# Reordering the work around one late load, and reading 64 bytes of every 64 KB of two weight matrices early

## The chip, the cores and the metric

The kernel runs on one core of one Trainium2 chip. The metric is the device time of one execution in microseconds (us), lower is better. Kernels are compared only within the same rounds.

## The reference

Eight batches of linear attention with a cosine weighting of positions, then one feed-forward layer with a gated activation. Only the shapes and the formulas matter here.

```python
q, k, v: (8, 8, 576, 64)      # batch, heads, sequence, head dim
r_c, r_s = relu(x) * cos(theta), relu(x) * sin(theta)      # phi(x) = [r_c, r_s]
kv  = einsum('bhsf,bhsd->bhfd', phi(k), v);  z = phi(k).sum(axis=2)
num = einsum('bhsf,bhfd->bhsd', phi(q), kv)
x   = num / (einsum('bhsf,bhf->bhs', phi(q), z) + 1e-6)    # -> (4608, 512)
h   = x @ w_in                        # w_in 512 x 2048
g   = h * sigmoid(beta * h)
out = g @ w_out                       # w_out 2048 x 512
```

## The kernel before

The tokens go through the feed-forward layer in nine chunks of 512. A chunk has 32 slots: 16 with the four matmuls of one h tile each, 16 with four output ("o") matmuls each. The attention of the next tokens is woven in between these slots. Chunk 0 is special: the weights are still being loaded, and batch 1's q, k and v arrive while it runs.

All loads but the small one of beta go through one queue (SyncE's) in this order: batch 0's q, v, k, the w_in blocks, then w_out blocks 0 to 7, batch 1's v, k and q, one DMA that transposes, and w_out blocks 8 to 15. TensorE's matmuls run in program order here, so one that waits holds up all behind it: in the hole of 1.13 us below, o matmuls that need nothing stand behind a turn that waits.

The parts that the change touches:

```python
    def kv_mm(b, jp, bank):       # 36 matmuls 64x64x130 into banks 6, 7
    def kv_take(jps, bank, eng):  # one copy PSUM -> kv, on ScalarE ("act") or VectorE
    def q_turn_pe(b, jp, bank, hold):   # 9 transposes on TensorE into bank, bank + 1
        ...
        # take("act", i): qt <- PSUM on ScalarE; take("dve", i): qs <- PSUM * tan on VectorE
    def num_mm(n, jp, bank, slot):      # 8 matmuls 64x64x65; num_seven is 7 of these
    def x_rden(...)                     # sum + eps and its reciprocal, VectorE
    def x_mul(got, n0, n1)              # the divide, one VectorE multiply
    def x_mul_act(got, n)               # the same as activations with a scale, ScalarE
    def cast_out(j, eng):               # w_out block j: fp32 stage -> bf16, times 1/beta

    # prologue, batch 0, second half of the heads
    got = x_rden(0, 0, 0, 7, (1,))
    x_mul(got, 0, 4)
    x_mul(got, 4, 7)
    x_mul(x_rden(6, 0, 7, 8, (1,)), 7, 8)
    for jt in range(3):
        h_mm(0, jt, (0, 1))
    x_turn_pe(0, 0, 4, 4, ("act",), (1,))
    # ... (cut)

    def second():                       # run after slot 23's o matmuls
        takes.append(q_turn_pe(1, 1, 6, hold=True))
        cast_out(8)
        takes[0]("act", 0); takes[0]("dve", 1)
        cast_out(9, "a")
        takes[0]("dve", 0); takes[0]("act", 1)
        cast_out(10)
        # ... takes[1] likewise (cut)
        cast_out(11, "a")
        cast_out(12)
        for j in range(13, JT):
            cast_out(j, "a")

    early = {                           # what runs after the matmuls of a slot of chunk 0
        # ... (cut)
        22: lambda: (kv_mm(1, 0, 6), kv_mm(1, 1, 6), kv_take((0, 1), 6, "act"),
                     takes.append(q_turn_pe(1, 0, 4, hold=True))),
        23: second,
        24: lambda: (num_seven(0, 4), x_mul(x_rden(4, 0, 0, 7, (0,)), 0, 7)),
        26: lambda: (num_seven(1, 6), x_mul(x_rden(6, 0, 0, 7, (1,)), 0, 7)),
        # ... (cut)
    }
```

The second q turn writes banks 6 and 7, which kv's product also used: it may start only when kv_take has read them.

## Time and profile before

| what | number |
|---|---|
| time, median of 3 runs | 295.02 us (294.88 to 295.82) |
| span in the profile | 293.1 us |
| TensorE busy | 282.5 us, 96% |
| batch 1's q lands | 39.49 us |
| TensorE's hole ahead of the first q turn | 1.13 us, 39.20 to 40.33 |
| first h matmul of chunk 1 ("c1") | 51.31 us |

The prediction below shows the page and the stretches. Two more views of the same trace matter for what follows. The first is ScalarE's timeline just after batch 1's kv product (start, length, engine, line, operation, output and input, count, and in brackets the idle time before it and who ended that). The kv product ended at 39.20 and the copy begins 0.11 us later:

```profile
39.31 0.59 ACT L269 CAST kv<-ps 128x520 bf16<-128x520 f32 x1 [1.98 <-PE ps L259]
```

The second is the chain of waits at the second num product (line 280; line 390 is the o matmuls). The 51 matmuls that the chain lists of this product run as one block, with no "issue" inside ("issue" is time in which the engine waited for nothing that the profile shows):

```profile
44.02 1.67 PE ps L390 x7
45.69 0.58 PE ps L280 x51
46.27 0.32 PE ps L390
```

**q** is the landing of batch 1's q; **P** is the first h matmul behind the transposes of the second half of the heads (the seventh h matmul in all), where TensorE's long full stretch in chunk 0 begins.

### The profile page before, as it was taken

The numbers are of one execution on the slowest core, as the hardware profiler recorded it, in microseconds if no ns is written. First come the engines' busy times: TensorE is split into PE (matmuls) and PEld (weight loads), VectorE is DVE, ScalarE is ACT, GpSimd is POOL, SyncE is SP. The second block draws the span as 40 slices with busy tenths as digits, with TensorE's granted clock in tenths as the row PEclk, the third lists the DMA queues.
The fourth block names the chain that finished last, engine by engine and source line by source line (L and its number), as shares of the span: only waits on it lengthen the run. The fifth ranks groups of instructions, "written<-read, shape, count | busy, mean of one in ns | idle before, by whom it ended". The sixth has DMA issues, their size and how long they took to land.

```text
span 293.1 us, 7188 instructions
## 1 busy us (share of the span) xinstructions
PE 282.5 (96%) x3046; PEld 143.2 (49%) x3073; DVE 115.0 (39%) x292; ACT 142.5 (49%) x226; POOL 73.3 (25%) x85
## 2 busy tenths in 40 slices
PE   8699989999999999999999999999999999999994
PEld 7454455455445544454445544554455444444444
DVE  5999976743910292029400950087005000000000
ACT  5768756862157324821474137512760277137511
POOL 1440000642381028202640255015701210000000
PEclk9999999999999999999999999999999999999999
DMA  7999999999999079906991699139102910131033
GB/s 259 369 394 382 392 292 389 290 250 341 162 262 352 5 147 236 400 12 130 220 386 58 121 221 394 57 65 188 54 2 53 142 36 0 38 83 24 0 74 72
DMA packets 50737, 53.89 MB, mean 184 GB/s; under 512 B 31233, under 2 KB 31633, under 8 KB 50705
## 3 DMA queue, kind: packets, MB, share of 16 engines
q1 hardware_dynamic: 47744, 45.95, 53.5%
q0 software_dynamic: 2688, 7.34, 10.4%
q8 instruction: 24, 0.39, 0.6%
q10 hardware_dynamic: 272, 0.14, 0.2%
q14 instruction: 9, 0.07, 0.1%
HBM read 36.71 MB, written 9.44 MB: 157 GB/s over the span
## 4 chain that ended last, share of the span: by engine, by line
PE 84%; DMA 8%; DVE 3%; issue 1%; SPq 1%
PE ps L390 39%; PE ps L365 38%; DMA raw_q<-in_q_dram 5%; PE ps L280 3%; DMA raw_v<-in_v_dram 3%; PE ps L259 2%; DVE win L108 2%; PE ps L408 1%; SPq L78 1%; DVE xs L302 1%; PE ps L229 0%; DVE vb L204 0%; DVE rden L295 0%; PE ps L339 0%; DVE qb L189 0%
## 5 line engine op out<-in xcount | busy, mean ns | idle before, releaser
L365 PE MATMUL ps<-xt,win 128*128 128x512 bf16 (+1 forms) x580 | 127.4, 378 | 0.1
L390 PE MATMUL ps<-wout,g_t 128*128 128x512 bf16 x535 | 120.4, 379 | 2.1 <-issue 1.1
L372 ACT ACTIVATE g_t<-ps,beta 128x512 bf16<-128x512 f32 x144 | 98.5, 688 | 33.3 <-PE ps L365 33.3
L365 PEld LDWEIGHTS <-win 128*128 128x128 bf16 x580 | 56.0, 98 | 66.1 <-DVE win L108 0.7
L390 PEld LDWEIGHTS <-g_t 128*128 128x128 bf16 x560 | 53.9, 98 | 63.6
L385 POOL DMA_DIRECT2D out_dram<-o_sb x56 | 37.2, 668 | 144.9 <-ACT o_sb L396 144.9
L396 ACT COPY o_sb<-ps 128x512 f32<-128x512 f32 x35 | 20.2, 587 | 98.2 <-PE ps L390 94.0
L271 DVE CAST kv<-ps 128x520 bf16<-128x520 f32 x6 | 4.2, 699 | 68.3 <-PE ps L259 68.3
L217 POOL TENSOR_TENSOR qs<-qt,tanr 128x1152 bf16<-128x1152 bf16 x12 | 28.4, 2382 | 7.2 <-DMA qt<-qb 6.4
L411 DVE COPY o_sb<-ps 128x256 f32<-128x256 f32 (+1 forms) x2 | 0.7, 358 | 62.9 <-PE ps L408 62.9
L302 DVE TENSOR_TENSOR xs<-ps,rden 128x768 bf16<-128x768 f32 (+5 forms) x27 | 23.1, 862 | 0.9
L291 DVE TENSOR_TENSOR den<-ps,eps 128x12 f32<-128x12 f32 (+4 forms) x26 | 4.2, 160 | 33.6 <-PE ps L280 33.5
L214 DVE TENSOR_SCALAR vb<-raw_v,cos 128x256 bf16<-128x256 f32 x63 | 17.1, 347 | 0.0
L214 DVE TENSOR_SCALAR vb<-raw_v,sin 128x256 bf16<-128x256 f32 x54 | 14.7, 347 | 0.0
L280 PEld LDWEIGHTS <-qt 64*64 64x64 bf16 x576 | 10.5, 106 | 4.7 <-issue 3.4
L280 PE MATMUL ps<-kv,qt 64*64 64x65 bf16 x576 | 11.7, 195 | 0.5 <-ACT kv L269 0.5
L189 DVE TENSOR_SCALAR qb<-raw_q 128x1152 bf16<-128x1152 f32 x16 | 11.4, 752 | 1.6 <-DMA raw_q<-in_q_dram 1.6
L259 PE MATMUL ps<-vb,rk 64*64 64x130 bf16 x576 | 10.2, 218 | 1.7 <-ACT rk L187 1.6
L280 PE MATMUL ps<-kv,qs 64*64 64x65 bf16 x576 | 11.5, 193 | 0.0
L108 DVE CAST win<-w_stage 64x512 bf16<-64x512 f32 x26 | 11.2, 433 | 0.6
L259 PEld LDWEIGHTS <-rk 64*64 64x64 bf16 x576 | 8.5, 106 | 5.6 <-issue 2.5
L189 DVE TENSOR_SCALAR rk<-raw_k 128x2304 bf16<-128x2304 f32 (+2 forms) x9 | 10.5, 1172 | 0.6 <-DMA raw_k<-in_k_dram 0.6
(59 smaller groups left out, 98.5 us busy)
## 6 DMA issues: line engine op xcount, KB each, us to landing
raw_v<-in_v_dram SPq DMA_DIRECT2D x7, 1152.0 KB, 10.5
raw_k<-in_k_dram SPq DMA_DIRECT2D x7, 1152.0 KB, 13.2
raw_q<-in_q_dram SPq DMA_DIRECT2D x7, 1152.0 KB, 7.4
out_dram<-o_sb POOLq DMA_DIRECT2D x56, 128.0 KB, 4.0
w_stage<-in_moe_w_in_dram SPq DMA_DIRECT2D x3, 1024.0 KB, 13.6
w_stage<-in_moe_w_out_dram SPq DMA_DIRECT2D x2, 1024.0 KB, 8.8
w_stage<-in_moe_w_out_dram SPq DMA_DIRECT2D x4, 512.0 KB, 11.2
out_dram<-o_sb SPq DMA_DIRECT2D x14, 128.0 KB, 2.3
```

Source lines behind the costliest of these rows:

```text
L108: nc.vector.tensor_copy(o, a)
L189: nc.vector.tensor_scalar(dst, src, scalar1=0.0, scalar2=None, op0=ALU.max)
L214: nc.vector.tensor_scalar(o, a, scalar1=t[:, n : n + 1], scalar2=None, op0=ALU.mult)
L217: eng.tensor_tensor(dst.rearrange("q n (g p) -> q n g p", g=2), src.rearrange("q n (g p) -> q n g p", g=2), tanr[:, n0:n1].unsqueeze(2).to ...
L259: nc.tensor.matmul(t[jj * HP : (jj + 1) * HP, g], lhsT=rk[hs, n, 2 * jp + jj, :], rhs=vb[hs, n, 2 * jp + jj].rearrange("q s e -> q (s e)") ...
L280: nc.tensor.matmul(ps[cols, bank + jj, slot * E : (slot + 1) * E], lhsT=(qt, qs)[cs][rows, jp, n, cols], rhs=kv[rows, g, jp, cs, :], start ...
L302: nc.vector.tensor_tensor(o.rearrange("q j n s d -> q j (n s) d"), nv[:, :, a:z, :, 0:D].rearrange("q j n s d -> q j (n s) d"), rden[:, :, ...
L365: nc.tensor.matmul(ps[:, h_bank(c, jt), blocks.start * 64 : blocks.stop * 64], lhsT=win[jt // 4][:, mi, (jt % 4) * P : (jt % 4 + 1) * P], ...
L372: nc.scalar.activation(g_t, ps[:, h_bank(c, jt)], AF.Silu, scale=beta[:, jt : jt + 1])
L385: eng.dma_start(out=out_v[bb, n][:, m0:m1], in_=o_sb[hf * HP : (hf + 1) * HP, m0:m1])
L390: nc.tensor.matmul(o_ps, lhsT=gs[c, jt][:, tt * P : (tt + 1) * P], rhs=wout[jt // 4][:, jt % 4, :], start=(jt == 0), stop=(jt == JT - 1))
L396: nc.scalar.copy(o_sb, o_ps)
```

## The change

The intent has two parts. In the order: slot 23's o matmuls need nothing of batch 1, so they go ahead of its kv product, and both q turns follow together; TensorE's hole in front of the first q turn is to be filled. One more slot of o matmuls goes ahead of the first num product, w_out's casts are dealt out anew, and one small divide goes to ScalarE. In memory: 64 bytes of every 64 KB of both weight matrices are read by GpSimd's queue in the first microseconds, so that a cost of touching the matrices first would be paid before their loads.

```diff
+    first = const.tile([64, 2, 16], FP32, name="first")
+    for i, w in enumerate((moe_w_in, moe_w_out)):
+        step = w.shape[0] // 64
+        nc.gpsimd.dma_start(out=first[:, i], in_=w.rearrange("(a b) f -> a b f", b=step)[:, 0, 0:16])
 # ... (cut)
     got = x_rden(0, 0, 0, 7, (1,))
+    x_mul_act(x_rden(6, 0, 7, 8, (1,)), 7)
     x_mul(got, 0, 4)
     x_mul(got, 4, 7)
-    x_mul(x_rden(6, 0, 7, 8, (1,)), 7, 8)
 # ... (cut)
     def second():
 
+        kv_mm(1, 0, 6)
+        kv_mm(1, 1, 6)
+        kv_take((0, 1), 6, "act")
+        takes.append(q_turn_pe(1, 0, 4, hold=True))
         takes.append(q_turn_pe(1, 1, 6, hold=True))
 # ... (cut)
-        cast_out(11, "a")
-        cast_out(12)
-        for j in range(13, JT):
+        for j in (11, 12, 14, 15):
             cast_out(j, "a")
 # ... (cut)
-        22: lambda: (kv_mm(1, 0, 6), kv_mm(1, 1, 6), kv_take((0, 1), 6, "act"),
-                     takes.append(q_turn_pe(1, 0, 4, hold=True))),
         23: second,
-        24: lambda: (num_seven(0, 4), x_mul(x_rden(4, 0, 0, 7, (0,)), 0, 7)),
+        25: lambda: (num_seven(0, 4), x_mul(x_rden(4, 0, 0, 7, (0,)), 0, 7), cast_out(13)),
```

## The prediction

> **What bounds the kernel now.** I read the page's first lines first, then the chain of work that ended last, then busy time by stretch, then the timeline around the one gap that the stretches show, and last the packet records of the first 60 us.
>
> The page of the kernel before, its span and engine rows:
>
> ```profile
> span 293.1 us, 7188 instructions
> PE 282.5 (96%) x3046; PEld 143.2 (49%) x3073; DVE 115.0 (39%) x292; ACT 142.5 (49%) x226; POOL 73.3 (25%) x85
> ```
>
> TensorE is busy 96% of the span; only 10.6 us are not matmul time. No change that leaves the matmuls alone can win more than that, and this one adds and removes none. Busy time by stretch shows where the 10.6 us lie (columns: stretch, its length, then busy us and count for PE, PEld, DVE, ACT, POOL, then granted clock, DMA share, GB/s):
>
> ```profile
> 0.00:16.50 16.50, 13.17 (x315) 10.77 (x318) 12.88 (x33) 11.00 (x24) 6.01 (x15) 1.00 0.89 324
> 16.50:19.00 2.50, 2.14 (x15) 0.98 (x15) 2.32 (x9) 1.08 (x2) 1.76 (x3) 1.00 1.06 394
> 19.00:37.98 18.98, 18.93 (x106) 8.71 (x105) 17.70 (x45) 14.85 (x26) 0.00 (x0) 1.00 1.10 377
> 39.20:40.33 1.13, 0.00 (x1) 0.00 (x0) 0.81 (x2) 0.59 (x1) 0.00 (x0) 1.00 0.93 298
> 40.33:47.00 6.67, 6.40 (x147) 3.92 (x151) 5.63 (x11) 4.60 (x8) 0.00 (x0) 1.00 1.05 383
> 52.70:293.10 240.40, 234.92 (x2331) 114.74 (x2348) 73.22 (x191) 106.46 (x161) 64.58 (x67) 1.00 0.57 146
> ```
>
> TensorE is full from 19.0 to 37.98, has one hole of 1.13 us (39.20 to 40.33), and is full again. From 52.7 on, the chain is TensorE work in a fixed rhythm of some 30.3 us per token chunk (52.72, 82.30, 112.65, 142.99), which the change doesn't touch. So the question is only **how many us earlier or later TensorE gets to 52.7**. The chain names what fills the hole (start, us, what):
>
> ```profile
> 24.08 15.41 DMA raw_q<-in_q_dram
> 39.49 0.02 issue
> 39.52 0.77 DVE qb L189
> 40.29 0.05 issue
> 40.33 0.68 PE ps L229 x9
> 41.01 0.05 issue
> 41.06 0.81 PE ps L390 x3
> 41.87 0.50 PE ps L229 x9
> 42.38 0.86 PE ps L390 x4
> ```
>
> Batch 1's q lands at 39.49, VectorE's ReLU takes 0.77, and only then can TensorE turn it. TensorE stands in program order behind that turn, though four output matmuls (the 0.81 piece) that need nothing from q come right after. Why does q land so late, 15.4 us after its issue? Because the SyncE queue is full: the stream moves 377 to 394 GB/s from 16.5 to 37.98. q is bound by bytes, not by its issue. One dent in this stream:
>
> ```profile
> 11.00:12.00 1.00, 0.70 (x36) 0.64 (x37) 0.84 (x3) 0.19 (x2) 0.00 (x0) 1.00 1.05 369
> 12.00:13.00 1.00, 0.71 (x64) 0.79 (x65) 1.00 (x1) 1.00 (x5) 0.97 (x1) 1.00 0.89 263
> 13.00:14.00 1.00, 0.01 (x2) 0.01 (x2) 0.92 (x6) 1.00 (x4) 0.28 (x1) 1.00 1.04 377
> ```
>
> 263 GB/s in the very us in which the first rows of w_in arrive. In the packet records some forty 2048-byte packets between 11.2 and 13.2 take 150 to 375 ns, where 83 is usual. This is what the 64-byte reads aim at: some cost of touching the matrix first. The loss is about (390 - 263)/390 x 1 us = 0.33 us; equally, the first half megabyte of w_in took 1.65 us between landings of the median engine and the second 1.36. **W_out shows no such dent**: 389, 379 and 393 GB/s from 22 to 25 us, where its first load runs.
>
> **What the Trainium skill says.** "DMA: Bandwidth & Descriptors", section "Issuing engines are not separate DMA queues": DMAs from any engine run on the same 16 DMA engines and interleave. So the new reads aren't free beside SyncE's stream, they share its engines. Nothing in the trace before contradicts it, but GpSimd issues no DMA before 51.75 us there, so it isn't tested in the part that matters. The same page, section "Why small descriptors are slow (HBM only)": each packet has a fixed cost, which 64 bytes can't spread. The trace's 512-byte packets of beta take about 20 ns each without load. "Runtime: NRT & Kernel Launch", section "Instruction fetch mechanics": instructions are refilled in 16 KiB blocks by a DMA. The trace agrees: single packets of 16,384 bytes, 962 to 1127 ns, at 9.7, 18.4 and 24.6 us. No page I found speaks of a first-touch cost of DRAM.
>
> **The change part by part.**
>
> *Part 1, the small reads.* Two DMAs of 64 descriptors of 64 bytes each. GpSimd has finished its identity tiles at 2.16 us and waits until 8.91 for v, so issuing two DMAs (668 ns each in the store row) from 2.2 to about 3.6 is free there. Nobody reads the tile. The cost is on the DMA engines: 128 packets and 32 semaphore writes over 16 engines, 10 each, at 20 to 30 ns is 0.2 to 0.3 us of each engine, more if each first touch itself costs 100 to 300 ns, at about 3 to 4.5 us, when q, v and k of batch 0 are streaming. The return is at most the 0.33 us of w_in's dent; for w_out nothing. All of it sits before batch 1's q in the same stream, so q's landing moves by cost minus return: **between -0.3 and +0.3 us, my guess -0.1.** In the prologue, which waits for v and k landings (8.76, 10.25, 11.96), the cost comes before the return, so its middle may be 0.2 later.
>
> *Part 2, block 7's divide.* It leaves VectorE's queue as an 0.29 us multiply at 18.53 and becomes two ScalarE activations, 0.30 each in the same form at 14.15. Its sum and reciprocal (0.15 and 0.17, with gaps 0.4) now run ahead of the two large multiplies, so the first transposes start about 0.4 later (18.2 in place of 17.83), but the last no longer waits at 18.88 for the small multiply. First xt copy: 18.65 to 19.23 for 18.26 to 18.84; second: about 19.25 to 19.83 for 19.15 to 19.73. So 0.1 us later for TensorE, and VectorE reaches the casts of the second w_in window about 0.25 earlier. Both are invisible at the end as long as TensorE waits for q at 40 us anyhow.
>
> *Part 3, order around the hole.* Slot 23's four output matmuls (0.86) go ahead of batch 1's kv; both q turns follow together; one more slot of output matmuls comes ahead of the first num products; VectorE's cast of block 12 goes to ScalarE and of block 13 later to VectorE. With q landing unchanged: output matmuls 37.98 to 38.84; kv (1.22) to 40.06; hole of 0.27 to the q ready at 40.33; first turn to 41.01; second turn to about 41.7, its ReLU being done at 40.95; slot 24 needs wout block 8, whose cast is
>
> ```profile
> 41.35 0.48 DVE L116 TENSOR_SCALAR wout<-w_stage,rbeta 128x512 bf16<-128x512 f32 x1 [0.40 <-DMA w_stage<-in_moe_w_out_dram]
> ```
>
> and ends at 41.83, because its data lands at 41.32. So slot 24 starts at 41.88: before it started at 42.38 with the same work done. **Gain here 0.50, or by idle time 1.13 - 0.27 - 0.15 = 0.71.** Is it given back? Slot 25 at 42.75; first num at 43.6, its tan products are ready at 43.17; slot 26 44.3 to 45.16; second num needs tan products that end at 44.88: fits by 0.3. Slot 28 at about 46.6 needs block 12 on ScalarE, landing 45.43 plus 0.72 is 46.2: fits. Block 13 on VectorE after the x multiply, about 46.4, for slot 29 at 47.9: fits. So the gain should reach 52.7.
>
> Sum: -0.6 (mean of the two) for the order, -0.1 for the stream: **-0.7 us, 294.3 us.**
>
> **The rivals.** *(a) The order gains nothing, a wait takes its place*: slot 24 would wait for w_out block 8, which sits behind q and a transpose in the same queue. For it: 41.32 is only 0.4 before need. Against: I counted it, 0.15. If it and the tan products each cost 0.3 more, the result is 294.8. *(b) The small reads slow the early stream*: misses of 0.3 us or more on each engine, in the time when q, v and k set the pace; for it: around v's first packets, at 5.6 to 5.8, some packets took 541, 726 and 1353 ns, and engines so delayed stay behind (q waits for the slowest). Then q lands 0.5 later, the gain is gone: 295.0. *(c) The reads do more than their dent*: if the laggard engines catch up, q lands 0.5 earlier, the hole closes fully (limit 1.13) and TensorE is bound from 19 on: 293.7. *(d) Nothing but TensorE counts*: the hole is 0.4% of the time, runs differ by 0.94 us (294.88 to 295.82); nothing to see.
>
> **Range and chances.** -0.7 with +-0.5 for the stream and +-0.3 for the waits, and the spread of medians about 0.3: **294.3, from 293.4 to 295.1** in 8 of 10. Faster by 2% needs -5.9 us, over half of all TensorE idle time, with one hole of 1.13 to win: chance 0.01. Slower by 2% needs a new stall of 5.9 us in a chain where every release has at most a few tenths to lose: 0.01. Within 2%: 0.98.
>
> **What would show it.** In the changed kernel's profile: the two small DMAs on GpSimd's queue near 2.2 to 3.6 us; the 12 to 13 us stretch near 380 GB/s if first touch was the cause, about 263 still if not; w_in's slow packets gone and some slow 64-byte ones near 3 to 4; q landing within 39.2 to 39.8; the hole before the first q turn at 0.3 or less; a new wait of 0.1 to 0.2 for wout's cast before slot 24; the first steady chunk's matmuls beginning 0.5 to 0.9 earlier than 52.72; the 30.3 us rhythm unchanged. It would be wrong if q landed over 0.5 later or earlier, if the second num waited for its tan products, or if the dent moved rather than vanished.

## The result

The changed kernel took **295.65 us** (median of 4 runs, 295.61 to 296.0), the kernel before 295.12 (4 runs, 294.88 to 295.82) in the same rounds. The ratio is **1.0017, with a 95% interval from 0.9998 to 1.0035**: the same within 2%, with a middle 0.2% above rather than below, and an interval that includes 1.

The page of the changed kernel's profile, first lines:

```profile
span 294.2 us, 7191 instructions
PE 282.5 (96%) x3046; PEld 142.4 (48%) x3073; DVE 114.3 (39%) x291; ACT 142.7 (48%) x228; POOL 68.3 (23%) x87
```

TensorE's busy time is 282.5 us as before, so again only its idle time is in question. Busy time by stretch (columns as in the prediction):

```profile
5.00:6.00 1.00, 1.00 (x16) 1.00 (x15) 0.97 (x4) 0.00 (x0) 0.00 (x0) 1.00 1.09 302
...
12.00:13.00 1.00, 0.67 (x64) 0.73 (x65) 0.00 (x0) 0.28 (x1) 0.00 (x0) 1.00 1.03 352
...
39.20:40.33 1.13, 1.13 (x21) 0.47 (x23) 0.18 (x1) 0.00 (x0) 0.00 (x0) 1.00 0.43 92
40.33:47.00 6.67, 5.89 (x194) 3.83 (x188) 6.20 (x12) 4.69 (x8) 0.00 (x0) 1.00 1.05 384
```

**The hole is filled**: from 39.20 to 40.33 TensorE is busy all 1.13 us. But the stretch behind it, to 47.00, has lost 0.51 us of busy time (5.89 against 6.40 before). And the dent in the stream at 12 to 13 us has shrunk, from 263 to 352 GB/s, while the stretch at 5 to 6 us has fallen to 302 (362 before, from the same view). Whether that is the reads' doing, two traces can't tell; the text after e8 comes back to it. The chain of waits of the changed kernel names what sits behind the hole (line 235 is the q turn, 265 kv's product, 275 kv's copy, 286 the num product, 396 the o matmuls):

```profile
40.18 1.15 PE ps L265 x72
41.33 0.40 PE ps L235 x5
...
41.76 0.60 ACT kv L275
...
42.40 0.66 PE ps L235 x9
...
46.33 0.18 PE ps L286 x6
46.51 0.21 issue
46.73 0.61 PE ps L286 x45
```

Two things are new. TensorE's second q turn waits for ScalarE's copy of kv, which begins only at 41.76 though the product ended at 41.33. And the second num product, which was one block before, is broken after its sixth matmul by 0.21 us of "issue"; from the start of one matmul to the start of the next it is 0.41 us.

GpSimd's two small DMAs are there, issued at 2.11 and 2.77 us and landed at 8.10 and 8.31. The table sets the two profiled runs side by side. It also shows that the two runs weren't given the same loads: v of batch 0 and q of batch 1 both landed later in the second.

| us | before | after |
|---|---|---|
| batch 0's v, second half, lands | 11.96 | 13.22 |
| P | 18.95 | 19.88 |
| batch 1's q lands | 39.49 | 40.13 |
| c1 | 51.31 | 52.38 |
| c1 minus P | 32.36 | 32.50 |
| c1 minus q | 11.81 | 12.24 |
| span minus c1 | 241.8 | 241.8 |

Of the 1.07 us by which c1 came later, 0.93 is the later P and 0.14 what lies between P and c1. In that part the hole of 1.13 us has gone, and three waits came: 0.5 more for casts of w_in (weight loads waited 0.9 us for them from 24 to 30 us, 0.4 before; a w_in load had landed only at 20.16), 0.47 for kv's copy, and 0.41 in the second num product. That is 1.38 for 1.13, or 0.25 more where 0.14 was measured. How much of this belongs to the change, and how much to these two runs, is what the experiments had to tell.

### The profile page after: what moved, and what is told of

The parts are those of the page before. It is cut to its first block, busy times and chain, and to the rows that moved or that the text cites. A ratio compares the mean times of both kernels' runs of the same rounds, so it can differ in the third digit from the quotient of the medians. Undisturbed runs are those within 1.5% of the kernel's fastest.

```text
span 294.2 us, 7191 instructions
## 1 busy us (share of the span) xinstructions
PE 282.5 (96%) x3046; PEld 142.4 (48%) x3073; DVE 114.3 (39%) x291; ACT 142.7 (48%) x228; POOL 68.3 (23%) x87
## 4 chain that ended last, share of the span: by engine, by line
PE 88%; DMA 6%; DVE 3%; issue 1%; ACT 0%; SPq 0%
PE ps L396 41%; PE ps L371 40%; DMA w_stage<-in_moe_w_in_dram 5%; PE ps L286 3%; PE ps L265 3%; DVE win L108 2%; DMA raw_q<-in_q_dram 2%; PE ps L414 1%; PE ps L235 0%; PE ps L345 0%; ACT kv L275 0%; SPq L78 0%; DVE xs L308 0%; DVE o_sb L417 0%; DVE rden L301 0%
## 5 line engine op out<-in xcount | busy, mean ns | idle before, releaser
L391 POOL DMA_DIRECT2D out_dram<-o_sb x56 | 31.1, 560 | 148.1 <-ACT o_sb L402 148.1
L308 DVE TENSOR_TENSOR xs<-ps,rden 128x768 bf16<-128x768 f32 (+4 forms) x26 | 22.8, 884 | 1.0 <-DVE rden L301 0.2
L286 PEld LDWEIGHTS <-qs 64*64 64x64 bf16 x576 | 10.5, 105 | 0.3 <-issue 0.3
```

Of the source, the lines that this page charges most:

```text
L286: nc.tensor.matmul(ps[cols, bank + jj, slot * E : (slot + 1) * E], lhsT=(qt, qs)[cs][rows, jp, n, cols], rhs=kv[rows, g, jp, cs, :], start ...
L308: nc.vector.tensor_tensor(o.rearrange("q j n s d -> q j (n s) d"), nv[:, :, a:z, :, 0:D].rearrange("q j n s d -> q j (n s) d"), rden[:, :, ...
L391: eng.dma_start(out=out_v[bb, n][:, m0:m1], in_=o_sb[hf * HP : (hf + 1) * HP, m0:m1])
```

## The experiments

Fourteen kernels ran, all with a correct result. The first twelve were timed in rounds against the kernel before; the last two were one look each, with a profile. **My first theory** was that the new order puts a wait for kv's copy where the hole was, and that the reads only cost. **The rivals**: the late loads of the run with the profile are chance; the reads are to blame for them; or something in TensorE's stream, not in the data, makes the pause in the num product.

### Taking the change apart: e1, e2, e3, e4

e1 is the change without the reads:

```diff
-    first = const.tile([64, 2, 16], FP32, name="first")
-    for i, w in enumerate((moe_w_in, moe_w_out)):
-        ...
```

> The changed kernel without the small reads (new order and block 7's divide on ScalarE stay). Theory A (the small reads cost the time: they leave one DMA engine about 1.3 us behind in the first 13 us, and the order gains): 0.5 to 0.8 us under the kernel before, v's second half lands near 12.0, q of batch 1 near 39.5. Theory B (the order itself gains nothing, because the wait for ScalarE's kv copy takes the place of the wait for q): within 0.2 us of the kernel before.

e2 is the kernel before with both reads; e4 with those of w_in alone:

```diff
+    first = const.tile([64, 2, 16], FP32, name="first")
+    for i, w in enumerate((moe_w_in, moe_w_out)):     # e4: (moe_w_in,)
+        ...
```

> The kernel before plus the small reads and nothing else. Theory A: v's second half lands about 1.2 us later (near 13.2), q of batch 1 near 40.1 in place of 39.49, and the time is 0.6 to 1.3 us over the kernel before. Theory B: the reads are harmless to the end, within 0.2 us.

> The kernel before plus the small reads of w_in alone (64 descriptors in place of 128). If each small packet or first touch costs the stream, half the damage of e2 (0.3 to 0.6 us over). If it is w_out's touches that do the damage, no loss or a gain of up to 0.3 us, w_in's slow packets near 12 us gone.

e3 is the kernel before with the new order and the new casts, but neither the reads nor the divide on ScalarE:

```diff
+    # second(): kv_mm, kv_mm, kv_take, q_turn_pe first, as in the change
-    22: lambda: (kv_mm(1, 0, 6), ...),
-    24: ...
+    25: lambda: (num_seven(0, 4), ..., cast_out(13)),
```

> The kernel before with the new order around batch 1's kv and q turns alone, no reads, divide as before. Theory A: 0.5 to 0.8 us under the kernel before, as e1, since the divide is hidden. Theory B: within 0.2 us. If the divide matters, e1 and e3 differ by over 0.2 us.

Measured against 295.01 us of the kernel before (11 runs of the same rounds):

| kernel | median us | ratio [95%] | q | P | c1 | c1 minus q | c1 minus P |
|---|---|---|---|---|---|---|---|
| e1 no reads | 295.10 | 0.9995 [0.9968, 1.0022] | 39.67 | 19.41 | 51.63 | 11.96 | 32.22 |
| e2 reads alone | 294.86 | 0.9998 [0.9969, 1.0027] | 39.20 | 19.47 | 50.99 | 11.80 | 31.52 |
| e3 order alone | 294.85 | 0.9990 [0.9964, 1.0017] | 39.16 | 18.84 | 50.92 | 11.76 | 32.07 |
| e4 reads of w_in | 294.75 | 0.9987 [0.9958, 1.0016] | 39.72 | 19.87 | 51.52 | 11.80 | 31.66 |

None of the parts can be told from the kernel before by its time: every interval includes 1. The traces tell more. **With the old order c1 is q + 11.80** (11.81 in the kernel before, 11.80 in e2, e4 and, below, e6), whatever P is: TensorE's chain hangs on q, as the prediction had it. **With the new order alone (e3) c1 is q + 11.76**: of the 0.50 to 0.71 us that the prediction gave the order, 0.04 is left, in a run without reads and with early loads. So the order failed by itself. Its chain shows a wait for w_out's block, and a slow restart behind it:

```profile
41.01 0.50 DVE wout L116
...
41.55 0.38 PE ps L390
...
41.98 1.46 PE ps L390 x6
```

TensorE stood 0.14 us for this cast, where the prediction had counted 0.15. But its first two matmuls then start 0.43 us apart (41.55 and 41.98), where 0.22 is usual. Why the restart was slower I have not found; e7 and e10 below wait for the same cast and don't show it. Later e3 has a pause of 0.31 us behind the fifth matmul of the second num product, and e1 one of 0.16. Both belong to the question of e13.

### Was the profiled run a bad draw? e5, e6, e7, e8

e5 is the changed kernel once more, without any edit.

> The changed kernel once more, unaltered. Theory C (the change is worth nothing either way: the reads only move the slow packets from w_in's arrival to q's, v's and k's, the order's gain is taken by the wait for the kv copy; runs differ by where the slow packets fall): within 0.3 us of the kernel before. Theory A (a real loss): 0.4 to 0.8 us over again. In its profile the wait of the second q turn for the kv copy (0.4 to 0.5 us) should be there again if TensorE reaches kv after q has landed.

e6 is the kernel before with the divide on ScalarE alone:

```diff
     got = x_rden(0, 0, 0, 7, (1,))
+    x_mul_act(x_rden(6, 0, 7, 8, (1,)), 7)
     ...
-    x_mul(x_rden(6, 0, 7, 8, (1,)), 7, 8)
```

> The kernel before with block 7's divide on ScalarE alone. The old order is set by q in all three traces (first matmul of chunk 1 at q's landing plus 11.80 us), so the divide can't show: within 0.2 us of the kernel before, chunk 1 at q plus 11.8. If the late start of the kv copy (0.38 us after its wait was over, seen in the two kernels with this divide) comes with the divide, it appears here too; if it comes with TensorE arriving late and without a gap, it doesn't.

e7 is the change without reads, and with kv's product and copy put back to slot 22, ahead of slot 23's o matmuls; both q turns stay together behind those:

```diff
     def second():
-        kv_mm(1, 0, 6)
-        kv_mm(1, 1, 6)
-        kv_take((0, 1), 6, "act")
         takes.append(q_turn_pe(1, 0, 4, hold=True))
 ...
+        22: lambda: (kv_mm(1, 0, 6), kv_mm(1, 1, 6), kv_take((0, 1), 6, "act")),
         23: second,
```

> The changed kernel without the reads, and with kv and its copy ahead of slot 23's output matmuls (as before the change), both q turns together behind them. The copy is then done long before the second turn. If the wait for the copy is what takes the order's gain: chunk 1 at q plus 11.5 to 11.7, or at the start of the continuous stretch plus 31.6 where that is later (32.2 and 32.5 in the traces with the new order), and 0.2 to 0.5 us under the kernel before. If the gain is lost elsewhere (casts of w_out, restart of the matmuls): q plus 11.8, within 0.2 us.

e8 is the kernel before with eight times as many 64-byte reads (1024 descriptors in place of 128):

```diff
+    first = const.tile([P, 2, 4, 16], FP32, name="first")
+    nc.gpsimd.dma_start(out=first[:, 0], in_=moe_w_in.rearrange("(p a) f -> p a f", a=4)[:, :, 0:16])
+    nc.gpsimd.dma_start(out=first[:, 1], in_=moe_w_out.rearrange("(p a r) f -> p a r f", a=4, r=4)[:, :, 0, 0:16])
```

> The kernel before with eight times as many small reads (64 bytes of every 8 KB of both matrices, 1024 descriptors). If small packets cost the stream: v's second half lands at 14 or later (11.8 to 12.0 without reads, 12.5 to 13.2 with 128), q at 40.5 or later, 1 us or more over. If only first touches cost, and one touch of each 64 KB has paid them all: as with 128 reads, within 0.3 us of the kernel before.

Measured against 294.84 us of the kernel before (11 runs):

| kernel | median us | ratio [95%] | q | P | c1 | c1 minus q | c1 minus P |
|---|---|---|---|---|---|---|---|
| e5 the change again | 295.07 | 1.0007 [0.9993, 1.0020] | 39.11 | 19.59 | 51.78 | 12.67 | 32.20 |
| e6 divide alone | 294.44 | 0.9985 [0.9973, 0.9998] | 38.98 | 18.53 | 50.78 | 11.80 | 32.25 |
| e7 kv first | 294.37 | 0.9982 [0.9967, 0.9996] | 39.21 | 18.79 | 50.66 | 11.45 | 31.88 |
| e8 reads x 8 | 295.67 | 1.0029 [1.0007, 1.0050] | 40.95 | 21.95 | 53.17 | 12.23 | 31.23 |

e5 settles the draw: q landed a full microsecond earlier than in the first profile of the same kernel (39.11 against 40.13), yet c1 came only 0.60 earlier. **With kv behind slot 23, TensorE hangs no longer on q but on P**: c1 is P + 32.20 to 32.50 in the three traces with this order and the divide (e1, e5, the changed kernel), and TensorE reaches the first q turn 1.08 to 1.74 us after q's landing, where the ReLU needs only 0.84. (e3, whose P of 18.84 was early, still came to the q turn at q + 0.84.) Moving 1.13 us of work out of the hole means that TensorE reaches the q turn later than q does, and from then on every lateness of the prologue counts. In the old order q's lateness hid it.

e7 is what tells the order apart. It fills the same hole with the same o matmuls, but keeps kv ahead of them, so that its copy has 0.86 us of o matmuls to hide behind. Slot 24 begins at q + 2.41, in the kernel before at q + 2.89: the 0.48 us are the 0.50 that the prediction had worked out. 0.35 of it is left at c1, and the time is 0.18% below the kernel before. The chain shows slot 24 and the first num product without a break:

```profile
41.62 1.89 PE ps L390 x8
43.50 0.58 PE ps L280 x56
```

So the idea of the hole was sound, and with kv in its new place the gain was lost. The pairs that differ in kv's place alone say so by their traces: c1 is q + 11.45 in e7 for 11.96 in e1, and q + 11.45 in e11 below for 11.76 in e3. By their times alone the pairs can't be told apart; the intervals overlap.

e8 shows that small reads aren't free: the early loads come over 2 us later in its trace (v at 14.38), and the time is 0.29% up. For 128 reads nothing like that can be shown. In the traces up to e12, v's landing is 11.92 to 13.22 in the five with both reads or w_in's, no matter which order, and 11.78 to 12.99 in the eight without; q's is 39.06 to 40.13 and 38.98 to 39.89. Both swing by about a microsecond from run to run.

What the reads do to the slow packets isn't shown either. Of the 2048-byte packets that carry w_in's first rows, 37 took over 150 ns in the kernel before; with reads it was 14, 12 and 11 (e2, e4, the change), but 23 and 38 in e10 and e5. Without any reads it was 22 in e1, 12 in e6, 28 to 49 in e3, e7, e9 and e11, and none in e12. The dent of the stream at 12 to 13 us goes with it: 258 to 275 GB/s in five traces without reads, but also

```profile
12.00:13.00 1.00, 0.62 (x64) 0.69 (x64) 0.22 (x1) 0.54 (x2) 0.17 (x1) 1.00 1.06 353
12.00:13.00 1.00, 0.92 (x65) 0.69 (x64) 1.00 (x1) 1.00 (x5) 1.00 (x1) 1.00 1.02 359
12.00:13.00 1.00, 0.55 (x36) 0.54 (x36) 0.82 (x2) 0.40 (x1) 0.00 (x0) 1.00 1.06 394
```

in e1, e6 and e12, which have none, where the changed kernel has 352 and e5, the same kernel, 290. e1 also has the low 5 to 6 us of the changed kernel, 304 GB/s. The first half of w_in landed at 13.54 to 13.87 us without, 13.58 to 13.79 with reads (median engine). **The number of slow packets changes from run to run, with or without the reads, and the matrix didn't come earlier.** One trace of the kernel before was too few to read a cost of the first touch from.

### What holds up kv's copy? e9, e10, e11

The copy of kv began 0.38 to 0.40 us after ScalarE's semaphore instruction ahead of it in the nine traces with the divide on ScalarE other than e9 (e10 and e12 to e14 among them), and 0.06 us after it in the six without. In the chain of the changed kernel the copy stands behind the q turn, whose first five transposes end just before it; but in e7 the turn comes later than the copy, and the lag is the same, so the turn isn't what it waits for. The divide adds two ScalarE instructions, by which the copy becomes the 64th of ScalarE's records in place of the 62nd. Theory: the delay belongs to a place in the stream. Rival: it belongs to the copy or to the divide. e9 is e1 with two more one-column activations near 4.6 us, by which the copy becomes the 65th (its trace has one semaphore instruction fewer):

```diff
     nc.scalar.activation(warm, zero_b, AF.Silu, scale=1.0)
+    nc.scalar.activation(warm, zero_b, AF.Silu, scale=1.0)
+    nc.scalar.activation(warm, zero_b, AF.Silu, scale=1.0)
```

> The changed kernel without the reads (the earlier run of it: chunk 1 at P plus 12.81 from the kv start, second turn stalled 0.48 us by the kv copy), with two more one-column activations on ScalarE near 3 us, where it has nothing to do. Theory D (the kv copy starts 0.38 us after its wait because of its place in ScalarE's instruction stream; with the divide it has moved by two instructions, and all five traces with the divide have the lag, all five without it don't): the lag is gone (0.06 us), the stall of the second turn falls from 0.48 to under 0.1, and chunk 1 starts at the stretch's start plus 31.6 to 31.9 in place of 32.2, 0.2 to 0.4 us of time. Theory E (the lag comes from TensorE's back-to-back work or from the divide's data): the lag stays at 0.38 to 0.40 and the stall at 0.46 to 0.48.

e10 is e7 with the reads, e11 is e7 with the divide back on VectorE:

> The best order so far (kv and its copy ahead of slot 23's output matmuls, no hole left to hide in) with the small reads put back. If the reads delay v's second half and so the start of TensorE's full stretch (by 0.3 to 0.9 us), nothing hides it now: 0.3 to 0.7 us over that order without reads, so at the kernel before or 0.2 over. If the reads are harmless: as without them, 0.3 to 0.6 under the kernel before.

> The same order without reads and without block 7's divide on ScalarE. If the order alone carries the gain: 0.3 to 0.6 us under the kernel before and chunk 1 at q plus 11.45. If it was the divide (its stretch starts 6.66 us after v's second half in place of 7.0): about 0.3 us worse than with it, so 0.0 to 0.2 under the kernel before.

Measured against 295.24 us of the kernel before (11 runs):

| kernel | median us | ratio [95%] | q | P | c1 | c1 minus q | c1 minus P |
|---|---|---|---|---|---|---|---|
| e9 two more ahead | 295.00 | 0.9996 [0.9980, 1.0012] | 39.89 | 19.50 | 51.82 | 11.93 | 32.32 |
| e10 kv first, reads | **294.31** | **0.9976 [0.9960, 0.9991]** | 39.06 | 18.58 | 50.49 | 11.43 | 31.91 |
| e11 kv first, no divide | 294.63 | 0.9986 [0.9967, 1.0006] | 39.20 | 19.13 | 50.65 | 11.45 | 31.52 |

In e9 the lag fell to 0.06 us and the gap between the two q turns from 0.48 in e1 to 0.14, where e3, which hardly waits for the copy, has 0.07. The divide is still on ScalarE, so **the lag belongs to the place in ScalarE's stream** and not to the divide or the copy; what is special about the place isn't shown. But the time stayed where it was, as the next wait took its place. ScalarE's timeline and TensorE's chain in e9:

```profile
41.02 0.59 ACT L271 CAST kv<-ps 128x520 bf16<-128x520 f32 x1 [3.23 <-PE ps L261]
```

```profile
42.23 0.50 DVE wout L116
...
42.77 1.89 PE ps L392 x8
```

Slot 24 now stood 0.45 us for the cast of w_out block 8, whose data had landed at 42.2, behind q and the transpose. Two waits lay side by side, and taking one away showed the other.

e10 and e11 confirm e7: with kv first, c1 is q + 11.43 to 11.45 in all three, with and without reads, with and without the divide. The chain of e10, from slot 24 on, has the two num products (line 286) as whole blocks:

```profile
41.44 1.89 PE ps L396 x8
43.32 0.58 PE ps L286 x56
43.90 0.97 PE ps L396 x4
44.87 0.58 PE ps L286 x51
```

With e10 the reads are harmless, 0.9976 beside 0.9982 of e7. The divide brings P nearer to the landing of v: of the traces with the full warm-up, P minus that landing is 6.66 us in six of the eight with it (7.42 in e5, whose clock was halved from 14.76 to 18.17 us, and 6.79 in e12) and 7.0 to 7.1 in five of the six without it (7.57 in e8, whose clock was halved too). So the transposes come 0.35 earlier, not 0.1 later. What this is worth in time isn't clear: e11, without the divide, can't be told from e7 and e10. **e10 is the version that beats both kernels**, the one before by 0.24% and, reckoned through that and not measured side by side, the changed one by 0.3 to 0.4%.

### A miss: e12

If slot 24 waits for w_out block 8, which stands behind the transpose in the queue, its load can go ahead of the transpose. e12 is e7 with that:

```diff
         load_raw(1, "q")
+        load_w("out", 2, 2)
         x_turn_dma(0, 8, 9)
-        load_w("out", 2, 2)
```

> The kv-first order with the divide and without reads, and with the third w_out stage loaded ahead of the small transposing DMA in SyncE's queue, to test whether slot 24's wait for w_out's block 8 (0.22 us at q plus 2.2 to 2.4 in the three kv-first traces, its data landing at q plus 1.83 behind the transpose) is what sets the time now. If it is: block 8 lands at q plus 1.3 to 1.5, the wait is gone, chunk 1 starts at q plus 11.0 to 11.3 (11.43 to 11.45 now) and the time is 0.6 to 0.9 us under the kernel before. If VectorE's chain of tan products or the turns set it: chunk 1 stays at q plus 11.4, 0.4 to 0.7 under.

It took 296.28 us (294.89 to 298.92) against 295.12: 1.0052 [1.0014, 1.0090], 0.5% slower. The wait for w_out was gone, as planned, but the chain had a new piece, by far the longest pause so far:

```profile
45.46 0.18 PE ps L280 x6
45.64 1.42 issue
47.06 0.61 PE ps L280 x45
```

It stands again behind the sixth matmul of the second num product. TensorE waits for no semaphore there that the profile shows. What fits is its own instructions. The Trainium skill, "Runtime: NRT & Kernel Launch", section "Instruction fetch mechanics", says that TensorE holds 2048 instructions and gets new ones in blocks of 16 KiB by a DMA of its own, at a cost "mostly hidden". The trace has 24 such packets on one queue in the whole execution, and the first eight start when TensorE has begun nearly the same numbers of recorded instructions in each trace so far, e12's fourth aside: about 217, 660, 760, 1075, 1355, 1470, 1730, 2040. The pause comes at number 1207 to 1217, behind the packet that starts at 1075. In the kernel before this packet starts at 42.52 and TensorE gets to the place 3.1 us later, with no pause. All fourteen traces sort by this time: in the eight without a pause TensorE starts the sixth matmul 2.70 to 3.15 us after the packet's start; in the six with one (the changed kernel, e1, e3, e5, e8, e12) it starts the last matmul ahead of the pause, the fifth or sixth, 0.83 to 2.62 us after it. In e3, the changed kernel and e12 TensorE goes on 2.66, 2.63 and 2.45 us after the packet's start. In e12 the packet started late, only at number 1200.

### Is it the instructions? e13, e14

These two test it. The kernel starts with warm-up matmuls: products of zeros that nobody reads. Leaving out 20 of the 58 narrow ones takes 40 instructions (a weight load and a matmul each) from the front of TensorE's stream and changes no other work. If the pause belongs to the num product, it stays behind the sixth matmul. If it belongs to the stream, it moves by 20 matmuls. e13 is the changed kernel with this edit, e14 is e12 with it:

```diff
-    warm_pe(58, 48)
+    warm_pe(38, 48)
```

> The changed kernel with 20 of its 58 narrow warm-up matmuls left out, so that TensorE's stream is 40 instructions shorter ahead of everything else. Theory refill (TensorE pauses where a new block of instructions begins, until that block has come by DMA): the place of the pause stays fixed in the stream, so it moves about 20 matmuls later, from behind the 6th matmul of the second num product to about the 26th, or has gone because TensorE gets there 0.2 to 0.3 us later. Rival theory (a wait that belongs to the second num product itself, a bank or a tan product): the pause stays behind the 5th or 6th matmul, 0.1 to 0.4 us.

> The order of e12 (w_out's block ahead of the transpose; pause of 1.42 to 1.62 us behind the 6th matmul of the second num product) with 20 of 58 warm-up matmuls left out. Theory refill: a pause of 1.0 to 1.5 us behind about the 26th matmul. Rival: it stays behind the 6th.

One look each, so of unknown state: 302.84 and 302.06 us, against 295.12 in the same call. I had expected the pause to move. I had not expected 7 us. The pause of 1.42 us in e14's second num product has gone altogether. In e13 one of 0.17 us is left in it, **behind the 26th of its 56 matmuls, where in the changed kernel it was behind the 6th**: moved by 20, as many as were left out. But both have **new pauses elsewhere**, in matmuls that had none. The chain of e13, in the prologue (batch 0's kv, line 265) and in chunk 1's num products:

```profile
14.01 0.78 PE ps L265 x33
14.79 2.42 issue
...
72.08 1.32 PE ps L286 x133
73.40 3.53 issue
```

In e14 the same two places have 1.98 and 2.98 us:

```profile
15.35 1.98 issue
...
73.23 2.98 issue
```

With each of these four pauses goes an instruction packet: it starts at 14.74 and 74.35 in e13, at 14.96 and 73.74 in e14, from 0.4 us ahead of TensorE's stop to 1 us behind it, where in the kernel before the same packets started at 9.68 and 67.78, long before their use. TensorE goes on 2.47, 2.58, 2.37 and 2.46 us after the packet's start. With the pauses in the num products of six kernels and of e13 that makes eleven, all from 2.4 to 2.75 us: **the pause is in TensorE's own supply of instructions, and from the start of the packet to the next instruction it takes about 2.5 us.** Why the first and the seventh packet were asked for so late in e13 and e14 isn't shown.

A second loss follows the first. The clock granted to TensorE is halved for 3.41 us behind the long pause in chunk 1, in e13 from 78.38 and in e14 from 76.69. Behind the pause in the prologue it is halved too, but that can't be put down to the pause alone: e5 and e8, without it, have such a piece there as well. Busy time by stretch of e13 (the number before the last two is the granted clock, 1.00 when full):

```profile
16.50:20.00 3.50, 2.79 (x77) 2.14 (x78) 0.68 (x5) 1.96 (x4) 1.30 (x2) 0.56 1.05 390
78.00:82.00 4.00, 4.00 (x12) 1.43 (x11) 4.00 (x12) 0.59 (x1) 1.52 (x2) 0.57 0.60 118
```

The Trainium skill, "TensorE: Matmul & The Clock Gate", section "Part 1: The HAM clock gate (the "warmup" mystery)", says that TensorE goes to half its clock after an idle window of about 3.4 us. The 0.57 agrees with the half; in e14 a pause of 2.98 us was enough. With the clock the sum for e13 nearly comes out: c1 is 1.40 later than in the changed kernel (53.78 against 52.38), and what follows c1 takes 247.3 us against 241.8, of which 3.5 is the pause and 4 x 0.43 = 1.7 the clock; 0.3 stays open.

## Why the prediction was wrong

The predicted 294.3 us lay 1.35 us below the 295.65 measured, and the range ended at 295.1. The class, within 2%, was right.

**The bound** was right: TensorE's busy time is the same to 0.1 us, everything happens before c1, and the old order hangs on q (q + 11.80 in four traces; 12.23 in e8, where TensorE came to kv only when q had landed).

**The hole** was right: it is filled, and where kv keeps its place (e7, e10, e11) slot 24 comes about 0.5 us earlier relative to q, for 0.50 predicted. The wait for w_out block 8, predicted at 0.15, measured 0.14 in e3, 0.19 in e10 and 0.22 in e7 and e11. (In the changed kernel's own run it isn't met: TensorE came 1.13 us later than q to the first q turn.)

**The step that failed** is the last one of part 3: "Is it given back? ... So the gain should reach 52.7." I checked the waits for w_out and for the tan products, and those fit: TensorE never stood for a tan product. Three terms were left out.
- The second q turn writes the banks that kv's copy has to read first. In the kernel before there were 2.5 us between kv's product and that turn. With kv directly ahead of both turns it has only the first turn's 0.68 and takes 0.59 plus its start; TensorE stood 0.46 to 0.48 us (changed kernel, e1, e5). 0.33 of it is a late start at one place of ScalarE's stream (0.38 against 0.06, shown by e9), which no view of the kernel before could show. The names of the banks showed that there was a wait to count, but not its size: in the prediction's schedule the copy would have ended at 40.76 (kv's end at 40.06, then 0.11 and 0.59), in time for the second turn at 41.01, as in e3.
- TensorE's instructions for the second num product came late by 0.16 to 0.41 us (0.41 in the changed kernel, 0.20 in e5, 0.31 in e3, 0.16 in e1). The order leaves less time between the start of the block's packet and its use, 2.2 to 2.6 us for 3.1; with kv kept in its place (e7, e10, e11) it is 2.7 to 2.8, and there is no pause. That it is the stream's supply is shown by e13, where the pause moved by 20 matmuls, and by the way all traces sort.
- "Both are invisible at the end as long as TensorE waits for q": true of the old order, and the change itself ends it. With the hole filled c1 is P + 32.2 to 32.5, and the prologue's lateness counts in full. That it was 0.93 us in the profiled run, the slowest of the four (296.0), is chance as far as the runs show; it was 0.64 in e5.

In the sum: of -0.50 to -0.71 for the order, e3 shows -0.04. There it is not the copy that takes the gain, but the slow restart behind w_out's cast (0.2) and the pause in the second num product (0.31).

**Rival (a)**, a wait in place of the one removed, was the one that came true, but I had named the two wrong waits for it.

**Part 1, the stream**, was given -0.1 with -0.3 to +0.3. q's landing, 40.13, was outside the 39.2 to 39.8 that I named. But e5, the same kernel, had 39.11, outside on the other side. The term was too small in its spread: q swings by about 1 us from trace to trace, 38.98 to 39.89 without reads and 39.06 to 40.13 with them. The mechanism, a cost of the first touch that the reads pay ahead, isn't shown: the dent was read from one trace, and three traces without reads have 353 to 394 GB/s there. That 128 reads cost anything isn't shown; that 1024 do is (e8). A small misreading of the trace besides: beta's 512-byte packets took mostly 25 ns, not about 20.

**Part 2, the divide**, was put at 0.1 us later for TensorE. It is 0.35 earlier, P minus v's landing being 6.66 for 7.0, and e6 was 0.15% faster with it (an interval that just excludes no change, one of twelve that were taken). How an earlier P gets to the end in an order that hangs on q isn't shown; q's own landing at 38.98 in e6, the earliest of all, would do it, and q swings as much without the divide.

**What stays open**: why q and v swing by a microsecond; why e3's restart behind the w_out cast took 0.2 us more than e7's; what delays ScalarE at the one place of its stream; and why the packets of e12, e13 and e14 were asked for so late.

## What to carry to other kernels

When a hole in front of a late load is filled by moving work, ask three things: which buffers the moved work shares with what now follows it directly, whose copy thereby loses its shelter, and which earlier lateness the hole had been hiding. Fill a hole with work that produces nothing the next steps wait for (here the o matmuls), and leave the producer (kv) where its copy has time.

"Issue" in a chain, with no wait beside it, in the midst of a run of short instructions, points to the instruction supply. It is tested cheaply by adding or taking away instructions far ahead: if the pause moves, it is that. And the number of warm-up instructions isn't free to choose: here 20 narrow matmuls fewer cost some 7 us, in the one run of each of two kernels.

## What the Trainium skill lacked or had wrong

- "Runtime: NRT & Kernel Launch", section "Instruction fetch mechanics", calls the cost of a block boundary "mostly hidden". Here it was 0.16 to 0.41 us in four traces of the new order, 1.6 in e12, and 2.0 to 3.5 in the prologue and chunk 1 of e13 and e14. The section has no latency; eleven pauses show 2.4 to 2.75 us from the start of the 16,384-byte packet (itself 0.9 to 1.2 us) to the next instruction. Nor does it say that the request can come as late as the stop itself, as at 14.74 and 74.35 us in e13.
- No page that I found has the ScalarE delay: 0.38 to 0.40 us from a semaphore instruction to the start of the next, the 64th that is recorded of its stream, in nine traces, 0.06 us where the same copy was the 62nd or 65th.
- "DMA: Bandwidth & Descriptors" has nothing on packets that are slow where a matrix is first read: 37 of w_in's first 2048-byte packets took over 150 ns in the kernel before, where 83 is usual, and from none to 49 in the other traces without reads. 64-byte reads ahead of them gave 11 to 38 and no earlier landing.
- "TensorE: Matmul & The Clock Gate", section "Part 1: The HAM clock gate (the "warmup" mystery)", gives about 3.4 us for the idle window. The clock was halved behind pauses of 3.53 us in e13 and of 2.98 us in e14. The page doesn't name a late instruction block as a cause of such a pause.
